# Moving two of the first loads of a four-layer attention kernel from SyncE's queue to ScalarE's

## The chip, the cores and the metric

The kernel runs on one core of one Trainium2 chip. The metric is the time of one execution on the device in microseconds (us); less is better. A core has five engines that work side by side and wait for each other through semaphores: TensorE (PE, matrix products; its weight loads are listed as PEld), VectorE (DVE), ScalarE (ACT), GpSimd (POOL) and SyncE (SP). Each takes its instructions in program order. In this kernel SP only issues DMA transfers. A transfer that an engine issues goes into that engine's queue (q1 for SP and q10 for ScalarE in the profile) and is carried out by the core's 16 DMA engines.

## The reference

The input x has 2048 rows of 512 numbers in bfloat16. Four layers follow one another, A, B, A, B, each as x = x + layer(layernorm(x)):

```python
def _A_ref(x, wqkv, w_phi, wo):            # 32 heads of 16
    q, k, v = split(x @ wqkv)
    pq, pk = q @ w_phi, k @ w_phi          # per head
    phi_q = concat(softmax(pq), softmax(-pq))
    phi_k = concat(softmax(pk), softmax(-pk))
    kv, z = phi_k^T v, sum(phi_k)
    return (phi_q kv / (phi_q z + 1e-6)) @ wo
...
def _B_ref(x, wqkv, wo):                   # window of 8 keys, every second one
    ...
    return (softmax(q kg / 4) vg) @ wo
```

Only the first 20 us or so matter for the change: layer norm of the first rows, and the preparation of layer A's weights.

## The kernel before, in words

The 2048 rows are cut into four blocks of 512 (`self.x[0]` to `self.x[3]`), and a block into four tiles of 128 rows. Every piece of work is a small function, put into a list with a stage and an engine by `step`. `run` then calls these functions in an order written out by hand: each word of the text `_ORDER` is a number, in base 36, of one list (the lists are numbered as they are first named), and stands for the next function of that list. So a word's place in `_ORDER` fixes where its instructions stand in their engine's queue. Places of two engines relative to each other in the text mean nothing, except that the tile buffers are handed out in this order, from the text `_SLOTS`.

What happens at the start, with the lines of the profile:

- **Loads** (`s_loads`). SP issues, one after the other: the first half of the key weights (`lraw(1, 0)`, L349, 256 KB, into the tile `wraw`), tiles 0 and 1 of x's first block (`lx0`, L337, 128 KB each), the second half of the key weights (`lraw(1, 1)`), the first half of the query weights (`lraw(0, 0)`), x's second block (`lx(1)`, L340, 512 KB), the second half of the query weights (`lraw(0, 1)`), tile 2 of x's first block, the value weights (`lv`, L343, 512 KB), tile 3, and later the rest. ScalarE issues one load in `setup`, behind its table load: the small tensor w_phi (L325, `phis`, 16 KB in runs of 32 bytes).
- **Products of zeros** (`warm`, L309). PE multiplies the zeroed tile `kvT` by itself 14 times: 11 times before its first real work, and three times between the first groups of real work. Nothing reads the result.
- **Folding w_phi into the weights** (`s_fold`). q @ w_phi is x @ (wq w_phi). So PE transposes the raw weights (`tr(pr)`, L386, eight transposes of 128x128 for each half), an engine copies the result to the tile `wT` (`ev`, L202 on DVE, L204 on ACT), PE multiplies it by the block-diagonal `PHI` (`mm(m)`, L396, four products for each m), and an engine copies that to `WA` (`ev2`, L202 or L204). Stage `fold1` does the key weights, `fold0` the query weights. `PHI` is made from `phis` on DVE (L274).
- **Layer norm** of the first block (`s_ln_first`, `s_norm`): DVE takes the statistics of a tile (`stat`, L515 and L516), ACT makes the reciprocal standard deviation (L450, L453), DVE or ACT applies it (L466, L468), PE transposes the tile (`pt`, L482), an engine copies the transposed tile out (L202 or L204).
- **Keys** (`s_a1`, `mk(t)`, L632): for each tile four products with the four 128-row pieces `WA[:, k]` of the folded key weights, so the fourth product of the first tile needs the last of the four copies by `ev2`. ACT takes the exponentials (L638).

PE's order there is: products 1 to 11, `fold1` transposes of the first half, products 12 and 13, `fold1` transposes of the second half, transposes of tile 0, product 14, `fold0` transposes of the first half, the 16 products by `PHI` of `fold1` with the transposes of tile 1 among them, `fold0` transposes of the second half, then `mk(0)` and `mk(1)`.

Of the kernel before, what the change touches and what calls it, by code (L numbers as in the profile page):

```python
# [60 lines left out]
8 2 i 2e 2p 23 i a i i 9 i i i i i i i 4e 1m i 0 0 f i e c j b 2 k 3 4 j o 1m l 3 m p 1n 0 i 1 n 1t o 1o q 1m 1p
r 0 1m 1u s 1m z z z 5 1m 1r 7 6 z 20 20 7 1q 1s 1t 21 21 t 20 20 1v 22 10 z 22 1t 7 1t 20 1w 22 t 11 24 24 13 u
12 16 12 1t t 15 1t v 12 12 22 x 18 14 1x d w w 1y 2c y 18 18 26 18 2d 1f 2d 2c 1z 2d 24 2d 27 17 19 18 1a 1b 21
1c 1d 22 21 22 39 1e 20 20 22 39 25 2c 3b 3a 3a 1f 3a 2d 3a 2f 2c 1f 1f 39 22 2f 2d 2g 1g 29 1f 2d 1j 2f 2d 7 1h
29 1i 1k 3a 29 2n 29 2i 2n 3c 2o 2o 2o 2k 2o 2k 2q 1l 2h 2n 2a 2k 2f 2n 2k 3a 2o 2j 24 2q 2r 2q 2o 2o 2o 29 2y
28 2y 2y 3c 2l 2z 2v 2z 2s 2z 2z 2k 2y 2z 39 36 31 2z 36 2z 3a 3b 36 36 2v 31 2v 37 2v 31 2t 36 2z 36 2b 2b 2b
2b 2m 2m 36 36 2m 3a 2w 2m 2v 33 34 32 31 3c 35 2q 3c 36 3b 2x g 2x 2u 2x 30 37 2x 36 38 38 38 38 3i 3c 3h 3c 39
3b 3a 3j 3k 3k 3k 3c 3d 3c 3e 3l 3b 3m 3d 3e 5h 3n 3m 3c 3e 3e 3l 5i 3o 3m 3q 3p 3m 3m 4f 3r 3m 3d 3l 5j 3e 3e
3s 3m 5i 3t 3m 3u 3m 3v 3d 3e 3e bd 5h 5m 5n 5k 5i 5l 5i 5i 3m 3d 3e 7c 5h 7d 5p 5i 5o 5i 5i 5r 3f 3g 3g 5q 5i
3f 3g 5i 3w 3f 3z 3x 3f 3g 5s 3y 7e 40 41 3g 7d 5u 5v 7f 5t 3g 41 42 41 41 44 3g 43 3g 43 5w 5x 5x 7f 45 46 43  # L70
43 47 43 7f 5y 3f 90 47 48 49 3g 4c 91 5x 41 4b 41 41 41 4a 92 5x 4d 60 91 4l 5z 61 5z 93 5z 4q 62 5z 4g 7d 4g
4g 4m 4q 63 5z 7d 4r 93 4i 4l 63 66 64 67 7g 4s 7j 65 7h 7i 4h 4j 7k bo 4n 4q 4q 4u 4w 91 7l 4t 7l 7l 7m 7l 7o
68 7n 7n 4l 7p 3h 7n 7q 4w 93 4v 7n 4v 91 4f 6a 7r 4o 6b 7n 6k 6f 69 4g 4k 4l 7r 6l 7s h 4w 6g 6k 6m 4p 6a 6c 6p
7t 7u 6a 6k 6f 6n 7v 4w 6k 6h 94 6r 6d 4x 4x b2 6r 4x 97 6o 98 4x 95 6f 69 7x 96 99 99 9a 4y 6i 99 7w 9b 6q 9c
6q 9d 9b 9b 99 9e 9b 6r 6a 6e 6f 6j 83 84 d4 6q 7y 9f 7y 9b 6r 6s 6s 6s 6s 9f 9h 9i 4y 9g 4w 8d 80 9j 7z 6t 6t
88 6s 83 89 6t 88 88 88 8a 8b 8f 8c 7y 6r 7x 4x 9l 6u 9k 6u 4y 6u 4w 6q 6u 83 85 83 86 87 81 9r 9w 7y 9w 9s 9x
4v 82 4v 9w 6v 9y 9z 4z a1 6v 4z 6v 6w 4z 8e 6v 4z 6y 9m 6x 6z 70 9n 70 70 71 72 73 70 9m 74 72 72 8e 9m 50 50
50 75 50 9o 72 51 9r 52 76 53 8f 54 55 72 9p 9w 76 8f 79 55 77 7a 9r 9t 55 58 78 7b 9u 55 9r 56 9m 8f 59 8g 57
5a 57 8e 8g a3 8g 8g 57 bz b0 8e 9q 57 9v a0 5b 57 8h a3 5b bz 8h a3 8g 5d c0 5e 5c 5f c0 c0 b0 c0 bz 8h b1 5g
b3 b1 8f b0 b1 b3 a2 b1 a4 c0 b1 a4 b1 a3 a4 a2 a4 b4 b5 a5 bz a5 8i 8i c0 8i a2 b3 a4 a2 c0 bx b6 c0 b3 a5 by  # L80
bx by by b0 b7 bx by by by a3 8i bx 8j 8j b1 8j 8l a6 8k 8j 8m b1 8n ap by aq aq ap a6 aq aq 8o 8o 8p by 8r 8o
8o 8q 8s 8q as 8t 8q as ap 8q au as ap a6 8u 8q a7 aq at 8u 8w aq bz a7 8v a7 aq aq 8x 8y 8z bx a9 a6 a7 a8 b8
aa as ax b8 ab ac ac c0 aw by ad ac ac b8 ax b8 ae be af av ah bb bb bb b9 ag ae bb b8 bf ae ae c1 ai bc bc ae
bc ar be ax bc bc bc bc bc ax ay ai aj ac ak am ac an ac al ac be bm ao bn bm bj bn bm bn bp ax bn bu bu bu c2
bu bj bj bn bg c2 c1 bm bn be az az bv bn az az ba bj ba ba bn bu bk bu ba bj bu bu c1 c2 c2 c2 c1 bp c2 bl bl
bh bl bu bq bp bp br bi bv bl bw bw bs bu iw bt bw bw c2 c7 c8 ix c9 c2 c9 c1 c2 c9 ca c3 cb iw cc cb fp c4 ca
fq c3 cd cb c4 ca cf ce cb cb cg cb c4 fr c4 ch cb cj e0 fq c3 fs fs ci cb cb c3 fs c5 c4 c4 c4 ck cb c4 cl e1
e2 cm c3 e1 e0 cp cn co e3 e1 e6 e4 e1 cq e5 e0 c4 e1 e1 c5 cq e8 e7 e1 e1 e9 ea cq e1 cr e1 eb cu h9 ee ct ec
ef fq cq fq ed eg cs cs cv cs cs ha eh eg ft hb fu fv eg ha hc hc fw hc eg fx fy fy cw el fy ei cs cw cy cx cq
cq d0 ej ek cq d1 cq ei fy d2 fz cz ei ei g3 df df em g1 df g0 ei em eo dh c6 da ep d3 en eq dg g2 di df dj g0  # L90
d5 ha d5 g0 d4 d6 da g0 g4 er dk d5 dk ha db g0 dc g4 es g6 hd d8 hh he da i7 dk d5 hf hg hi dl g5 g7 d7 d9 i7
g8 hi hj dd hi hl hk hk hm hi hn hk hk ho hk ho hp et hr f3 eu et da ey dl ev ey ey hs de hq dl f4 f1 et dl ez
ey ht ew f2 f0 f3 f5 f3 dm g9 f8 dm dm f6 dm dn dk i1 dn fa i1 fa i2 i3 dl i6 i6 gq f3 f7 f9 es i6 i9 et i6 i9
i6 i6 f9 dm hu ex fa ga i9 ia dn id i6 hv i1 fb fb fa fb fb fc i4 i1 i5 i6 dl c6 i6 do fc i9 ie ib i6 do hw hx
do fb gg i6 f9 fc gl i6 i6 i6 gm i6 ic hu i8 dp i6 ic dp dr dp dq gh ds ic hw f9 gg gg ic gi hy ic ic gl ic gl
ic fa gn gb ic ic do fd fd c5 ic go ic ic hw hw ic hz gb fd ic dp gc fe i0 gj gs fe gd fe if dt ff if if fh ig
gb if ig gg ig gl gs ge gs fg ig gk gb gp gt gr gr gr gt ga gf ih ih if ig if ig du gr if if gs ih du ig dv gt
ii gt dw fd ig ij ij ii ik gu gu ij du gt du ij dy ik ih gu fe gs dz il gv fi gv ii ij ij im ik il fj fk fj dx
in fl iq fj ir fj dx fo iq fm is ii gw gw ij gv il ij gx ik gw il io gv gv fn fm iy gz iq ip iq iu it gy iv it
h2 gw h0 gw h2 iz h3 h4 h5 h3 h1 h2 h6 h3 h2 h3 h5 h7 h5 h8 iy h5 j0  # L100
"""


# [33 lines left out]
class _Fast:  # L137
# [177 lines left out]
    def setup(self):  # L315
        nc, const = self.nc, self.const
        nc.scalar.preload_act_table_set("natural_log_exp_and_others")
# [4 lines left out]
        self.phis = const.tile([P, NB, DH], BF16, name="phis")
        self.x = [const.tile([P, 4, D], BF16, name="x%d" % b) for b in range(4)]
        with nc.allow_non_contiguous_dma(reason="tiny w_phi load"):
            nc.scalar.dma_start(out=self.phis[:], in_=self.A_w_phi.rearrange("(hb hl) d f -> (hl d) hb f", hb=NB))  # L325
# [4 lines left out]

    def s_loads(self):
        nc, add = self.nc, self.step
        wav = self.A_wqkv.rearrange("(m p) c -> p m c", p=P)
        xv = self.A_x.rearrange("b (j p) d -> p (b j) d", p=P)

        def lx0(t):
            nc.sync.dma_start(out=self.x[0][:, t, :], in_=xv[:, t, :])  # L337

        def lx(b):
            nc.sync.dma_start(out=self.x[b][:], in_=xv[:, 4 * b:4 * b + 4, :])  # L340
# [4 lines left out]
        def lraw(qk, h):
            if qk not in self.wraw:
                self.wraw[qk] = self.med([NB, D], "wraw")
            c = qk * D + h * 256
            nc.sync.dma_start(out=self.wraw[qk][:, :, h * 256:(h + 1) * 256], in_=wav[:, :, c:c + 256])  # L349
# [1776 lines left out]
```

## Time and profile before

| | |
|---|---|
| three runs | 319.18, 319.34, 319.43 us, median 319.34 us |
| the profiled execution | 319.68 us, its span (first to last instruction) 317.9 us |
| PE busy | 307.5 us (97%) |
| DVE busy | 295.1 us (93%) |
| ACT busy | 275.2 us (87%) |
| POOL busy | 47.1 us (15%) |
| DMA | 36.37 MB, mean 114 GB/s |

The profile is one execution. A line of its time line gives start and length in us, the engine, the line of the program, the operation, the tile written and the tiles read, the count, and in brackets how long the engine had been idle before it and what ended the wait. `SPq` and `ACTq` are the issues of transfers by SyncE and ScalarE; the transfer itself lands later. Lengths of matrix products are modelled and overlap: 11 products of 0.63 us stand in 4.88 us.

### The profile page before, as it was taken

Reading aid. Unit: us, or ns where it says so; the run is one execution under the profiler, and the core shown is the slowest. Engines: PE = TensorE matmul, PEld = TensorE weight load, DVE = VectorE, ACT = ScalarE, POOL = GpSimd, SP = SyncE. Lnnn points to the kernel's source line nnn. Section 1 sums busy time; section 2 is a strip of 40 time slices with the busy share of each in tenths; the row PEclk is TensorE's granted clock in tenths of the full one; section 3 lists DMA queues with packets and bytes.
Section 4 is the critical chain, followed back from the end, with each engine's and each line's share of the span. In section 5 each row is a group of like instructions: output and inputs, shape, how many; then the busy total and the mean of one; then the engine's idle time right before and its main releaser. Section 6 shows DMA issues by size and latency. Waiting matters only on the chain.

```text
span 317.9 us, 8896 instructions
## 1 busy us (share of the span) xinstructions
PE 307.5 (97%) x3578; PEld 153.0 (48%) x3578; DVE 295.1 (93%) x459; ACT 275.2 (87%) x639; POOL 47.1 (15%) x60
## 2 busy tenths in 40 slices
PE   8999999899999999999999999988999999999994
PEld 4654456445454444444444455544454544444552
DVE  6999996898999999999999999699998999999994
ACT  3999999999888778999999999899999867788761
POOL 6000000000003212000000000027011644045000
PEclk9999999999999999999999999999999999999999
DMA  6986200005694989569895500005189885565954
GB/s 199 345 203 143 41 2 4 2 19 142 150 191 96 157 141 139 99 106 151 140 131 71 69 0 2 4 19 134 49 195 137 134 157 119 103 181 122 163 148 170
DMA packets 45789, 36.37 MB, mean 114 GB/s; under 512 B 30832, under 2 KB 41136, under 8 KB 45744
## 3 DMA queue, kind: packets, MB, share of 16 engines
q1 hardware_dynamic: 45216, 35.75, 56.5%
q8 instruction: 29, 0.48, 0.7%
q14 instruction: 16, 0.13, 0.2%
q10 hardware_dynamic: 528, 0.02, 0.1%
HBM read 11.13 MB, written 3.25 MB: 45 GB/s over the span
## 4 chain that ended last, share of the span: by engine, by line
PE 88%; ACT 5%; DVE 2%; DMA 2%; SPq 1%; issue 1%; DVEq 0%; ACTq 0%
PE PS L967 23%; PE PS L553 18%; PE PS L632 9%; PE PS L644 9%; PE PS L737 6%; PE PS L1128 4%; PE PS L1066 4%; PE PS L1185 2%; DMA wraw<-in_A_wqkv_dram 2%; PE PS L707 2%; ACT Eq L745 2%; PE PS L482 1%; PE PS L940 1%; PE PS L556 1%; PE PS L1200 1%; PE PS L1082 1%
## 5 line engine op out<-in xcount | busy, mean ns | idle before, releaser
L967 PE MATMUL PS<-xnT,WB 128*128 128x512 bf16 x336 | 76.6, 380 | 0.0
L1059 DVE TENSOR_TENSOR prod<-QT,K 128x4096 bf16<-128x4096 bf16 x28 | 63.3, 2285 | 0.5 <-POOL K L993 0.5
L1121 DVE TENSOR_TENSOR pav<-PT,Vg 128x4096 bf16<-128x4096 bf16 (+1 forms) x29 | 62.9, 2213 | 0.2
L967 PEld LDWEIGHTS <-WB 128*128 128x128 bf16 x336 | 37.3, 114 | 36.3 <-issue 3.1
L745 ACT ACTIVATE Eq<-PS 128x512 bf16<-128x512 f32 x64 | 36.3, 619 | 0.0
L638 ACT ACTIVATE Ek<-PS 128x512 bf16<-128x512 f32 x64 | 35.1, 623 | 0.2 <-PE PS L632 0.2
L553 PEld LDWEIGHTS <-oT 128*128 128x128 bf16 x236 | 21.9, 98 | 26.6 <-issue 1.3
L737 PE MATMUL PS<-xnT,WA 128*128 128x512 bf16 x128 | 32.0, 380 | 0.5 <-DVE s L829 0.3
L578 ACT ACTIVATE sqd<-x 128x512 bf16<-128x512 bf16 x48 | 30.0, 635 | 2.1 <-DVE x L571 2.0
L644 PE MATMUL PS<-WA,xnT 128*128 128x512 bf16 x128 | 31.6, 379 | 0.0
L571 DVE SCALAR_TENSOR_TENSOR x<-PS,x 128x512 bf16<-128x512 f32 x46 | 30.1, 683 | 0.7 <-PE PS L553 0.7
L632 PE MATMUL PS<-WA,xnT 128*128 128x512 bf16 x128 | 30.7, 379 | 0.0
L204 ACT CAST oT<-PS 128x512 bf16<-128x512 f32 (+1 forms) x50 | 26.8, 600 | 3.6 <-PE PS L1128 2.1
L553 PE MATMUL PS<-WoA,oT 128*128 128x512 bf16 x128 | 29.8, 380 | 0.0
L553 PE MATMUL PS<-WoB,oT 128*128 128x512 bf16 x108 | 26.5, 379 | 0.0
L204 ACT CAST K<-PS 128x512 bf16<-128x512 f32 x30 | 17.3, 594 | 3.0 <-PE PS L967 1.9
L632 PEld LDWEIGHTS <-xnT 128*128 128x128 bf16 x128 | 12.4, 98 | 14.8 <-issue 0.4
L644 PEld LDWEIGHTS <-xnT 128*128 128x128 bf16 x128 | 12.3, 98 | 14.4 <-issue 0.4
L690 DVE TENSOR_TENSOR Ek<-Ek,rk 128x4096 bf16<-128x4096 bf16 (+1 forms) x10 | 18.6, 1859 | 0.4 <-ACT rk L685 0.4
L737 PEld LDWEIGHTS <-WA 128*128 128x128 bf16 x128 | 11.7, 98 | 14.6 <-issue 1.7
L466 DVE TENSOR_SCALAR xn<-x,rstd,nmr 128x512 bf16<-128x512 bf16 x48 | 17.5, 412 | 0.5
L204 ACT CAST V<-PS 128x512 bf16<-128x512 f32 x26 | 15.2, 596 | 2.9 <-PE PS L967 2.9
(175 smaller groups left out, 506.4 us busy)
## 6 DMA issues: line engine op xcount, KB each, us to landing
Vg<-V SPq DMA_DIRECT2D x112, 131.5 KB, 4.7
Prho<-rd SPq DMA_DIRECT2D x8, 512.0 KB, 5.3
x<-in_A_x_dram SPq DMA_DIRECT2D x3, 512.0 KB, 6.8
WB<-in_B_wqkv_dram SPq DMA_DIRECT2D x3, 512.0 KB, 9.6
out_dram<-x SPq DMA_DIRECT2D x6, 256.0 KB, 2.3
wraw<-in_A_wqkv_dram SPq DMA_DIRECT2D x4, 256.0 KB, 4.2
vd<-Vs SPq DMA_DIRECT2D x2, 272.0 KB, 3.0
x<-in_A_x_dram SPq DMA_DIRECT2D x4, 128.0 KB, 3.6
```

The source lines that it names most:

```text
L204: self.nc.scalar.copy(out=out, in_=in_)
L553: nc.tensor.matmul(y[:], lhsT=lh(t, c), rhs=Wo()[:, c, :], start=(c == 0), stop=(c == NB - 1 and not onpe))
L571: nc.vector.scalar_tensor_tensor(out=xb[:, t, :], in0=T[t][:], scalar=1.0, in1=xb[:, t, :], op0=ALU.mult, op1=ALU.add, **kw)
L578: nc.scalar.activation(out=sqd[:], in_=xb[:, t, :], func=ACT.Square, accum_out=T["ss"][:, t:t + 1])
L632: nc.tensor.matmul(pk[:], lhsT=xnT[:, t, k, :], rhs=self.WA[:, k, D:2 * D], start=(k == 0), stop=(k == NB - 1))
L638: nc.scalar.activation(out=T["E"][:, t, s, :], in_=T["k", t][:], func=ACT.Exp, scale=1.0 - 2.0 * s)
L644: nc.tensor.matmul(pv[:], lhsT=xnT[:, t, k, :], rhs=self.WA[:, k, 2 * D:3 * D], start=(k == 0), stop=(k == NB - 1))
L737: nc.tensor.matmul(pq[:], lhsT=self.WA[:, k, hb * P:(hb + 1) * P], rhs=xnT[:, :, k, :], start=(k == 0), stop=(k == NB - 1))
L745: nc.scalar.activation(out=self.Eq[L, b][s][:, :, hb, :], in_=T[hb][:].rearrange("p (t i) -> p t i", t=4), func=ACT.Exp, scale=1.0 - 2.0 * s)
L967: nc.tensor.matmul(pp[:], lhsT=self.WB[:, k, i * D + c:(i + 1) * D:NB], rhs=xnT[:, :, k, :], start=(k == 0), stop=(k == NB - 1))
L1059: nc.vector.tensor_tensor(out=pr[:], in0=QT[:, c:c + 1, :].to_broadcast([P, NW, TB]), in1=win, op=ALU.mult)
L1121: nc.vector.tensor_tensor(out=pv, in0=PT[:, :, lo:lo + n].unsqueeze(1).to_broadcast([P, NB, 2, n]), in1=vw, op=ALU.mult)
```

## The change

Two loads are issued by ScalarE, behind the load of w_phi, and no longer by SP: tile 0 of x's first block, and the second half of the key weights. The load of w_phi itself moves from `setup` to a step of its own, and is still ScalarE's first transfer. SP's other loads stay in their order and close up.

```diff
+    "raw_act": ((1, 1),),
...
-        with nc.allow_non_contiguous_dma(reason="tiny w_phi load"):
-            nc.scalar.dma_start(out=self.phis[:], in_=self.A_w_phi.rearrange("(hb hl) d f -> (hl d) hb f", hb=NB))
...
+        def lphi():
+            with nc.allow_non_contiguous_dma(reason="tiny w_phi load"):
+                nc.scalar.dma_start(out=self.phis[:], in_=self.A_w_phi.rearrange("(hb hl) d f -> (hl d) hb f", hb=NB))
+
         def lx0(t):
-            nc.sync.dma_start(out=self.x[0][:, t, :], in_=xv[:, t, :])
+            q = nc.scalar if t == 0 else nc.sync
+            q.dma_start(out=self.x[0][:, t, :], in_=xv[:, t, :])
...
-            nc.sync.dma_start(out=self.wraw[qk][:, :, h * 256:(h + 1) * 256], in_=wav[:, :, c:c + 256])
+            q = nc.scalar if (qk, h) in _OPT["raw_act"] else nc.sync
+            q.dma_start(out=self.wraw[qk][:, :, h * 256:(h + 1) * 256], in_=wav[:, :, c:c + 256])
...
         for t in range(4):
-            add("ld_x0", "SP", lx0, t)
+            add("ld_x0", "SP" if t else "ACT", lx0, t)
+        add("ld_phi", "ACT", lphi)
...
-                    add("ld_raw%d" % qk, "SP", lraw, qk, h)
+                    add("ld_raw%d" % qk, "ACT" if (qk, h) in _OPT["raw_act"] else "SP", lraw, qk, h)
```

The whole text `_ORDER` changes, since three lists are new and every number behind them grows. Read back into steps, what differs is this:

- The first loads stand at the head of the text. ScalarE: w_phi, tile 0, second half of the key weights. SP: first half of the key weights, tile 1, first half of the query weights, x's second block, second half of the query weights, tile 2, value weights, tile 3, and on as before.
- PE: ten products of zeros (not eleven) stand before the `fold1` transposes of the first half, one (not two) between these and the transposes of the second half, and two behind them, before the transposes of tile 0. All 14 are still there.
- The order of every other step on its engine is as before. The text `_SLOTS` has one letter at another place, so that the second `wraw` tile, which is now named earlier, gets the buffer that it had.

More of the change, by code (lines that the diff above doesn't have):

```diff
@@ L60 @@
 _ORDER = """
[L61 to L100, printed above, removed]
+2 4 0 1 5 6 7 6 1 3 b l 2h 2s 26 l d l l c l l l l l l 4h 1p l i h f m e n m r 1p l l o p s 1q l q 1w r 1r t 1p
@@ new lines @@
+1s u 1 1p 1x v 1p 12 12 12 8 1p 1u a 9 12 23 23 a 1t 1v 1w 24 24 w 23 23 1y 25 13 12 25 1w a 1w 23 1z 25 w 14 27
+27 16 x 15 19 15 1w w 18 1w y 15 15 25 10 1b 17 20 g z z 21 2f 11 1b 1b 29 1b 2g 1i 2g 2f 22 2g 27 2g 2a 1a 1c
+1b 1d 1e 24 1f 1g 25 24 25 3c 1h 23 23 25 3c 28 2f 3e 3d 3d 1i 3d 2g 3d 2i 2f 1i 1i 3c 25 2i 2g 2j 1j 2c 1i 2g
+1m 2i 2g a 1k 2c 1l 1n 3d 2c 2q 2c 2l 2q 3f 2r 2r 2r 2n 2r 2n 2t 1o 2k 2q 2d 2n 2i 2q 2n 3d 2r 2m 27 2t 2u 2t 2r
+2r 2r 2c 31 2b 31 31 3f 2o 32 2y 32 2v 32 32 2n 31 32 3c 39 34 32 39 32 3d 3e 39 39 2y 34 2y 3a 2y 34 2w 39 32
@@ new lines @@
+39 2e 2e 2e 2e 2p 2p 39 39 2p 3d 2z 2p 2y 36 37 35 34 3f 38 2t 3f 39 3e 30 j 30 2x 30 33 3a 30 39 3b 3b 3b 3b 3l
+3f 3k 3f 3c 3e 3d 3m 3n 3n 3n 3f 3g 3f 3h 3o 3e 3p 3g 3h 5k 3q 3p 3f 3h 3h 3o 5l 3r 3p 3t 3s 3p 3p 4i 3u 3p 3g
+3o 5m 3h 3h 3v 3p 5l 3w 3p 3x 3p 3y 3g 3h 3h bg 5k 5p 5q 5n 5l 5o 5l 5l 3p 3g 3h 7f 5k 7g 5s 5l 5r 5l 5l 5u 3i
+3j 3j 5t 5l 3i 3j 5l 3z 3i 42 40 3i 3j 5v 41 7h 43 44 3j 7g 5x 5y 7i 5w 3j 44 45 44 44 47 3j 46 3j 46 5z 60 60
+7i 48 49 46 46 4a 46 7i 61 3i 93 4a 4b 4c 3j 4f 94 60 44 4e 44 44 44 4d 95 60 4g 63 94 4o 62 64 62 96 62 4t 65
@@ new lines @@
+62 4j 7g 4j 4j 4p 4t 66 62 7g 4u 96 4l 4o 66 69 67 6a 7j 4v 7m 68 7k 7l 4k 4m 7n br 4q 4t 4t 4x 4z 94 7o 4w 7o
+7o 7p 7o 7r 6b 7q 7q 4o 7s 3k 7q 7t 4z 96 4y 7q 4y 94 4i 6d 7u 4r 6e 7q 6n 6i 6c 4j 4n 4o 7u 6o 7v k 4z 6j 6n 6p
+4s 6d 6f 6s 7w 7x 6d 6n 6i 6q 7y 4z 6n 6k 97 6u 6g 50 50 b5 6u 50 9a 6r 9b 50 98 6i 6c 80 99 9c 9c 9d 51 6l 9c
+7z 9e 6t 9f 6t 9g 9e 9e 9c 9h 9e 6u 6d 6h 6i 6m 86 87 d7 6t 81 9i 81 9e 6u 6v 6v 6v 6v 9i 9k 9l 51 9j 4z 8g 83
+9m 82 6w 6w 8b 6v 86 8c 6w 8b 8b 8b 8d 8e 8i 8f 81 6u 80 50 9o 6x 9n 6x 51 6x 4z 6t 6x 86 88 86 89 8a 84 9u 9z
@@ new lines @@
+81 9z 9v a0 4y 85 4y 9z 6y a1 a2 52 a4 6y 52 6y 6z 52 8h 6y 52 71 9p 70 72 73 9q 73 73 74 75 76 73 9p 77 75 75
+8h 9p 53 53 53 78 53 9r 75 54 9u 55 79 56 8i 57 58 75 9s 9z 79 8i 7c 58 7a 7d 9u 9w 58 5b 7b 7e 9x 58 9u 59 9p
+8i 5c 8j 5a 5d 5a 8h 8j a6 8j 8j 5a c2 b3 8h 9t 5a 9y a3 5e 5a 8k a6 5e c2 8k a6 8j 5g c3 5h 5f 5i c3 c3 b3 c3
+c2 8k b4 5j b6 b4 8i b3 b4 b6 a5 b4 a7 c3 b4 a7 b4 a6 a7 a5 a7 b7 b8 a8 c2 a8 8l 8l c3 8l a5 b6 a7 a5 c3 c0 b9
+c3 b6 a8 c1 c0 c1 c1 b3 ba c0 c1 c1 c1 a6 8l c0 8m 8m b4 8m 8o a9 8n 8m 8p b4 8q as c1 at at as a9 at at 8r 8r
@@ new lines @@
+8s c1 8u 8r 8r 8t 8v 8t av 8w 8t av as 8t ax av as a9 8x 8t aa at aw 8x 8z at c2 aa 8y aa at at 90 91 92 c0 ac
+a9 aa ab bb ad av b0 bb ae af af c3 az c1 ag af af bb b0 bb ah bh ai ay ak be be be bc aj ah be bb bi ah ah c4
+al bf bf ah bf au bh b0 bf bf bf bf bf b0 b1 al am af an ap af aq af ao af bh bp ar bq bp bm bq bp bq bs b0 bq
+bx bx bx c5 bx bm bm bq bj c5 c4 bp bq bh b2 b2 by bq b2 b2 bd bm bd bd bq bx bn bx bd bm bx bx c4 c5 c5 c5 c4
+bs c5 bo bo bk bo bx bt bs bs bu bl by bo bz bz bv bx iz bw bz bz c5 ca cb j0 cc c5 cc c4 c5 cc cd c6 ce iz cf
@@ new lines @@
+ce fs c7 cd ft c6 cg ce c7 cd ci ch ce ce cj ce c7 fu c7 ck ce cm e3 ft c6 fv fv cl ce ce c6 fv c8 c7 c7 c7 cn
+ce c7 co e4 e5 cp c6 e4 e3 cs cq cr e6 e4 e9 e7 e4 ct e8 e3 c7 e4 e4 c8 ct eb ea e4 e4 ec ed ct e4 cu e4 ee cx
+hc eh cw ef ei ft ct ft eg ej cv cv cy cv cv hd ek ej fw he fx fy ej hd hf hf fz hf ej g0 g1 g1 cz eo g1 el cv
+cz d1 d0 ct ct d3 em en ct d4 ct el g1 d5 g2 d2 el el g6 di di ep g4 di g3 el ep er dk c9 dd es d6 eq et dj g5
+dl di dm g3 d8 hd d8 g3 d7 d9 dd g3 g7 eu dn d8 dn hd de g3 df g7 ev g9 hg db hk hh dd ia dn d8 hi hj hl do g8
@@ new lines @@
+ga da dc ia gb hl hm dg hl ho hn hn hp hl hq hn hn hr hn hr hs ew hu f6 ex ew dd f1 do ey f1 f1 hv dh ht do f7
+f4 ew do f2 f1 hw ez f5 f3 f6 f8 f6 dp gc fb dp dp f9 dp dq dn i4 dq fd i4 fd i5 i6 do i9 i9 gt f6 fa fc ev i9
+ic ew i9 ic i9 i9 fc dp hx f0 fd gd ic id dq ig i9 hy i4 fe fe fd fe fe ff i7 i4 i8 i9 do c9 i9 dr ff ic ih ie
+i9 dr hz i0 dr fe gj i9 fc ff go i9 i9 i9 gp i9 if hx ib ds i9 if ds du ds dt gk dv if hz fc gj gj if gl i1 if
+if go if go if fd gq ge if if dr fg fg c8 if gr if if hz hz if i2 ge fg if ds gf fh i3 gm gv fh gg fh ii dw fi
@@ L101 @@
+ii ii fk ij ge ii ij gj ij go gv gh gv fj ij gn ge gs gw gu gu gu gw gd gi ik ik ii ij ii ij dx gu ii ii gv ik
+dx ij dy gw il gw dz fg ij im im il in gx gx im dx gw dx im e1 in ik gx fh gv e2 io gy fl gy il im im ip in io
+fm fn fm e0 iq fo it fm iu fm e0 fr it fp iv il gz gz im gy io im h0 in gz io ir gy gy fq fp j1 h2 it is it ix
+iw h1 iy iw h5 gz h3 gz h5 j2 h6 h7 h8 h6 h4 h5 h9 h6 h5 h6 h8 ha h8 hb j1 h8 j3
 """
@@ L113 @@
     "med": (
-        "b79ca642352f85de6b0464b12833892cb7516e70efd8561f1706ed4a53bc7430e3f9eba731d9c0411a4091d20483b8ae4cf4"
+        "b679ca42352f85de6b0464b12833892cb7516e70efd8561f1706ed4a53bc7430e3f9eba731d9c0411a4091d20483b8ae4cf4"
         "b71d6236f9ec40bfd6ea7830c4"
```

## Prediction

> **What bounds the kernel now.** First the chain of waits of the whole span, then the same chain in order of time for the first 40 us.
>
> ```profile
> PE 88%; ACT 5%; DVE 2%; DMA 2%; SPq 1%; issue 1%; DVEq 0%; ACTq 0%
> ```
>
> ```profile
> 0.92 0.46 SPq L349
> ...
> 4.01 6.41 DMA wraw<-in_A_wqkv_dram
> 10.43 0.05 issue
> 10.47 0.62 PE PS L386 x8
> ```
>
> Past 10.47 us the chain is nearly all PE. Before it stand SP's issues one behind the other and then one transfer, the second half of the query weights, issued at 4.01 and landed at 10.43. So whatever moves this start should move the end by as much: nothing later in the chain hangs on an outside clock. Next, the time line of each engine.
>
> ```profile
> 0.92 0.46 SPq L349 DMA_DIRECT2D wraw<-in_A_wqkv_dram  x1
> 1.42 0.97 SPq L337 DMA_DIRECT2D x<-in_A_x_dram  x2
> 2.44 0.98 SPq L349 DMA_DIRECT2D wraw<-in_A_wqkv_dram  x2
> 3.46 0.51 SPq L340 DMA_DIRECT2D x<-in_A_x_dram  x1
> 4.01 0.51 SPq L349 DMA_DIRECT2D wraw<-in_A_wqkv_dram  x1
> ```
>
> ```profile
> 0.88 1.28 ACT L317 ACT_TABLE_LOAD   x1 [0.88 <-PEq L2110]
> 0.91 0.48 ACTq L325 DMA_DIRECT2D phis<-in_A_w_phi_dram  x1
> 5.50 0.29 ACT L450 ACTIVATE lnv<-mv,eps_t 128x1 f32<-128x1 f32 x1 [3.35 <-DVE mv L516]
> ...
> 8.82 0.59 ACT L204 CAST WA<-PS 128x512 bf16<-128x512 f32 x1 [0.30 <-PE PS L396]
> ...
> 9.78 1.58 ACT L204 CAST WA<-PS 128x512 bf16<-128x512 f32 x3
> 11.21 1.07 ACT L204 COPY wT<-PS 128x1024 bf16<-128x1024 bf16 x1
> ```
>
> ```profile
> 4.56 0.69 DVE L515 BATCH_NORM_STATS2 stat<-x 128x6 f32<-128x512 bf16 x1 [1.75 <-DMA x<-in_A_x_dram]
> ...
> 6.96 0.66 DVE L202 COPY wT<-PS 128x1024 bf16<-128x1024 bf16 x1
> ...
> 7.72 0.69 DVE L202 COPY wT<-PS 128x1024 bf16<-128x1024 bf16 x1
> ```
>
> ```profile
> 1.34 4.88 PE L309 MATMUL PS<-kvT 128*128 128x512 bf16 x11 [1.34 <-DVE kvT L264]
> 6.01 0.78 PE L386 MATMUL PS<-ident,wraw 128*128 128x128 bf16 x8
> 6.63 0.59 PE L309 MATMUL PS<-kvT 128*128 128x512 bf16 x2
> 7.06 0.61 PE L386 MATMUL PS<-ident,wraw 128*128 128x128 bf16 x8
> 7.73 0.38 PE L309 MATMUL PS<-kvT 128*128 128x512 bf16 x1
> ...
> 9.01 0.83 PE L396 MATMUL PS<-PHI,wT 128*128 128x128 bf16 x12
> 10.47 0.62 PE L386 MATMUL PS<-ident,wraw 128*128 128x128 bf16 x8 [0.63 <-DMA wraw<-in_A_wqkv_dram]
> 10.93 1.89 PE L632 MATMUL PS<-WA,xnT 128*128 128x512 bf16 x8
> ```
>
> Two separate chains meet at PE near 10.5 us. One is the transfer above: PE was through at 9.84 (9.01 + 0.83) and idled 0.63 us for it. The other starts when **tile 0 of x lands**: DVE, idle for 1.75 us, begins at 4.56 and is then busy nearly throughout (5.08 of the 5.50 us from 4.90 on, in the table below), and its copies of `wT` (to 8.41) let PE make the folded weights, which ACT copies out from 8.82 until 11.36 (9.78 + 1.58) without a pause. The second chain is nearly as late as the first. A key product is one seventh of 1.89 - 0.38 us, 0.216 us, behind the one before, so the fourth, the first that needs ACT's last copy, starts at 10.93 + 3 x 0.216 = 11.58. ACT was done at 11.36: 0.22 us of slack, 0.18 if 0.04 us are left for the signal (10.43 to 10.47 above).
>
> **The change part by part.** *SP's issues close up.* SP's issues stand 0.5 us apart (0.92, 1.42, then two from 2.44). Two of those ahead of 4.01 go to ScalarE, so the second half of the query weights is issued about 1.0 us earlier, at 3.0. Does it land 1.0 earlier? The DMA engines in stretches:
>
> ```profile
> core 0: us, PE busy (x) PEld busy (x) DVE busy (x) ACT busy (x) POOL busy (x), PEclk, DMA share, GB/s
> 2.60:3.20 0.60, 0.60 (x3) 0.30 (x2) 0.20 (x3) 0.00 (x0) 0.45 (x3) 1.00 1.12 284
> 3.20:3.80 0.60, 0.60 (x3) 0.15 (x1) 0.00 (x0) 0.00 (x0) 0.48 (x3) 1.00 1.18 311
> 3.80:4.90 1.10, 1.10 (x4) 0.46 (x3) 0.34 (x1) 0.00 (x0) 0.87 (x5) 1.00 0.68 194
> 4.90:10.40 5.50, 4.95 (x55) 3.44 (x52) 5.08 (x13) 3.98 (x10) 1.77 (x10) 1.00 1.03 323
> ```
>
> They are full except from 3.80 to 4.90, where they move 194 GB/s instead of 311 and are 0.68 busy. The bytes ahead of this transfer are the same after the change, so what can be won is that hollow: 1.1 x (1 - 194/311) = 0.41 us. Bounds: nothing, if the hollow stays; 1.0, if the issue alone decided. I take 0.40, the row with the rates being the nearest: landing at 10.03, transposes from 10.07.
>
> A rule speaks against even this. The Trainium skill, "DMA: Bandwidth & Descriptors", section "Issuing engines are not separate DMA queues", says that transfers issued by several engines run on the same 16 DMA engines and interleave, and that only the issuing time is saved. By it the gain lies in the hollow and nowhere else. The trace agrees where the share is 1.03; it shows no run with two busy queues.
>
> *Tile 0 of x on ScalarE's queue.* ScalarE issues w_phi at 0.91 while its table load runs, so at 0.5 us a piece tile 0 goes out at 1.4, when SP issued it before, and the second key half at 1.95 instead of 2.44. ScalarE has nothing else until 5.50 (idle 3.35 us), so the two issues themselves cost nothing. What changes is what stands ahead of the tile: no longer 256 KB of key weights, but w_phi's 528 small packets.
>
> ```profile
> q10 hardware_dynamic: 528, 0.02, 24.7%
> ```
>
> This is ScalarE's queue from 2.6 to 3.8 us (packets, MB, share of 16 engines): w_phi's whole transfer lies there, starting 1.7 us after its issue. Call d the shift of the tile's landing. Before, its bytes were the last 128 KB of about 384 KB and done near 3.7 (the 284 and 311 GB/s rows), 0.86 us before DVE started. If it may now follow w_phi's first packets, 1.4 + 1.7 = 3.1 and 128 KB at 311 GB/s (0.42 us) give 3.5: d = -0.2. If it starts when w_phi is half through, near 3.3, and shares the engines with tile 1 from SP, it needs twice 0.42 us: 4.1, d = +0.4. If it waits for w_phi's last packet at 3.8 and shares, 4.64: d = +0.9. I take +0.1, midway between the first two; the third needs the worst on every DMA engine.
>
> *What PE makes of both.* The transposes start at the later of 10.07 and PE's being free, 9.84 + d, so 0.40 us earlier. The fourth key product needs ACT's last copy, 11.36 + d, plus 0.04; it stood at 11.58. So PE's shift is the larger of -0.40 and d - 0.18, which for d = +0.1 is -0.08 us. ACT's copy of `wT` at 11.21 shifts by d as well and ends at 12.28 + d, before PE needs it at 12.66 (10.93 + 8 x 0.216). If this cover of 0.38 us were used up, d would be paid in full from there on.
>
> *The product of zeros.* The first transposes start one product earlier, at 5.6 (4.88 us for 11, 0.43 us each). The `wT` copy that waits for them stands at 6.96 behind DVE's own work, and the transposes are over at 6.79 already: worth nothing. The other transposes end at 7.67, the copy stands at 7.72: that cover is thin, and coming earlier only helps if d is negative. They may start near 6.7 if their half has landed:
>
> ```profile
> DMA to landing us min/median/max: 3.2/4.2/6.4
> ```
>
> By the median of the four weight halves it lands at 1.95 + 4.2 = 6.15, by the longest at 8.4, which would cost 0.7 us through that copy; the longest belongs to the half issued last, into the fullest queue, so I take the median and no cost. Tile 0's transposes get two products ahead of them in place of two plus the eight transposes: nothing.
>
> *Sum.* 319.68 for the profiled execution, less 0.08: 319.60. That execution lies 0.34 above the median of 319.34, so the forecast for the median is 319.26, told as 319.3. A quarter of a per mille is far inside 0.2% (0.64 us), which is about what a measurement of this kernel can tell from no change.
>
> **The rivals.** *Faster, tile 0 lands early.* If ScalarE's queue is served beside SP's from the first packet at 2.6, the tile's bytes are there by about 3.05, and d is -0.65. Then PE's shift is bounded by its own chain and the landing: with the landing moved by the whole 1.0 to 9.4, PE free at 9.2, the larger of -1.03 and -0.83: 318.5. For it: DVE's 1.75 us of idle time. Against it: w_phi's packets lie ahead in the same queue, and the DMA engines are full from 2.6 on. Both gains must be near their ends together; below d = -0.46 it would pass 0.64.
>
> *Slower, tile 0 behind w_phi.* This is the third case above: d = +0.9, all of DVE's and ACT's chain late by that, PE late by 0.72, and 320.1. It decides from d = +0.82. For it: the last of w_phi's packets run until 3.8, and tile 1 and two weight halves compete from both queues. Against it: w_phi takes 24.7% of the engines in that stretch, 0.3 us of each if it runs alone.
>
> *Slower, TensorE's clock.* Eleven products ran 0.43 us apart, the two at 6.63 only 0.21 (0.59 - 0.38). So PE doubles its pace near 6.4 us, while the first transposes run. After the change those stand half a microsecond further ahead. If this put the doubling off, PE would have four products and 40 transposes or small products left at half pace; 4 x 0.21 plus 40 x 0.056 (0.61 - 0.22 over seven steps) is 3.1 us at full pace, so up to 3.1 more, and nothing if the doubling came at once. I take the middle less the 0.4 of waiting for the weights, about 1.2: 320.6. The granted clock stands at 1.00 in every row and doesn't show this step. The rule of the Trainium skill, "TensorE: Matmul & The Clock Gate", Part 4, that a transpose doesn't count as busy time as a product does, is what would bring it about; the doubling in this trace came during transposes, but behind five microseconds of products.
>
> **How the numbers follow.** Forecast, no change: 0.62. Tile 0 early: 0.20. Tile 0 behind w_phi: 0.10. Clock: 0.08. So faster 0.20, same 0.62, slower 0.18. Within the forecast d from -0.3 to +0.5 gives 318.9 to 319.7. The range goes on to the fast rival at 318.5, with half of that case above it, and just below the slow one, 320.0; about one case in ten is left out at each side.
>
> **What would show it.** SP's issue of the second query half near 3.0, and its transposes at 10.0 to 10.1. DVE's first statistics near 4.7, and ACT's last copy of the folded key weights near 11.5, with the fourth key product waiting for it. The first transposes at 5.6, still followed by products 0.21 us apart. The hollow between 3.8 and 4.9 filled. I am wrong if DVE starts before 4.1 or after 5.3, if products after the first transposes are still 0.43 apart, or if the shift at 12 us is not found again at the end.

## The result, and the profile after

| | before | after |
|---|---|---|
| median (range), six runs each on the same chip | 319.39 us (319.18 to 319.60) | 322.48 us (321.64 to 323.46) |
| ratio, 95% interval | | 1.0096 [1.0079, 1.0113] |
| the profiled execution, its span | 319.68 us, 317.9 us | 323.04 us, 321.3 us |

The changed kernel is slower by 3.1 us. The forecast of 319.3 us is wrong, and so is the range, which ended at 320.0.

Its chain of waits by engine, and then the same chain in order of time:

```profile
PE 77%; DVE 9%; ACT 8%; DMA 2%; issue 2%; ACTq 0%; DVEq 0%
```

```profile
1.42 0.60 ACTq L341
...
2.05 6.81 DMA wraw<-in_A_wqkv_dram
8.86 0.05 issue
8.91 0.68 PE PS L392 x8
9.59 0.85 PE PS L310 x2
```

The transfer in the chain is no longer the second half of the query weights (landed at 10.43 us before) but the second half of the key weights. ScalarE issued it at 2.05 us and it landed 6.8 us later, at 8.86; on SP's queue it had been issued at 2.44 and had landed 4.1 us later, and its transposes had started at 7.06 without a wait. The time line, with the edited lines a few numbers further down than before:

```profile
0.91 0.48 ACTq L337 DMA_DIRECT2D phis<-in_A_w_phi_dram  x1
1.42 0.60 ACTq L341 DMA_DIRECT2D x<-in_A_x_dram  x1
2.05 0.46 ACTq L354 DMA_DIRECT2D wraw<-in_A_wqkv_dram  x1
...
2.99 0.51 SPq L354 DMA_DIRECT2D wraw<-in_A_wqkv_dram  x1
...
5.23 0.69 DVE L521 BATCH_NORM_STATS2 stat<-x 128x6 f32<-128x512 bf16 x1 [2.42 <-DMA x<-in_A_x_dram]
...
5.58 0.78 PE L392 MATMUL PS<-ident,wraw 128*128 128x128 bf16 x8
6.19 0.38 PE L310 MATMUL PS<-kvT 128*128 128x512 bf16 x1
...
8.91 0.68 PE L392 MATMUL PS<-ident,wraw 128*128 128x128 bf16 x8 [2.34 <-DMA wraw<-in_A_wqkv_dram]
9.38 1.06 PE L310 MATMUL PS<-kvT 128*128 128x512 bf16 x2
...
10.24 0.63 PE L488 MATMUL PS<-ident,xn 128*128 128x128 bf16 x4
...
13.74 0.61 PE L392 MATMUL PS<-ident,wraw 128*128 128x128 bf16 x8
...
14.72 1.73 PE L638 MATMUL PS<-WA,xnT 128*128 128x512 bf16 x7 [0.37 <-ACT WA L205]
```

PE idles 2.34 us for the second half of the key weights. Behind it the two products of zeros start 0.43 us apart (1.06 less the 0.63 of a single one), where the two at 6.63 us before stood 0.21 apart: PE works at half pace. The key products start at 14.72, 3.8 us later than the 10.93 of before. The stretches of the changed kernel show the clock and the DMA engines:

```profile
core 0: us, PE busy (x) PEld busy (x) DVE busy (x) ACT busy (x) POOL busy (x), PEclk, DMA share, GB/s
3.80:4.90 1.10, 1.10 (x4) 0.45 (x3) 0.00 (x0) 0.00 (x0) 0.87 (x5) 1.00 1.08 319
...
9.00:9.50 0.50, 0.50 (x9) 0.50 (x9) 0.00 (x0) 0.00 (x0) 0.00 (x0) 0.83 1.09 383
9.50:12.50 3.00, 3.00 (x22) 2.18 (x21) 1.32 (x3) 0.59 (x1) 0.00 (x0) 0.50 1.06 330
12.50:13.00 0.50, 0.50 (x9) 0.50 (x8) 0.50 (x2) 0.38 (x1) 0.00 (x0) 0.76 1.01 338
13.00:13.50 0.50, 0.50 (x11) 0.49 (x9) 0.48 (x1) 0.50 (x2) 0.00 (x0) 1.00 1.00 264
```

First row: the hollow of the DMA engines is filled as forecast, 319 GB/s instead of 194. The others: the granted clock is 0.50 from 9.33 (0.83 in a half microsecond is a third of it at 0.50) to 12.74, which is 3.4 us. In the profile of before, the rows of the same stretch show 1.00.

Why did the half take so long on a shorter queue? The packets of the two queues in two stretches, 4.25 to 6.00 us and then 6.00 to 8.75 us, and last those of ScalarE's queue alone from 7.65 to 8.50 us (packets, MB, share of 16 engines):

```profile
q1 hardware_dynamic: 525, 0.30, 58.0%
q10 hardware_dynamic: 476, 0.24, 49.0%
...
q1 hardware_dynamic: 1185, 0.92, 100.9%
q10 hardware_dynamic: 74, 0.04, 4.3%
...
q10 hardware_dynamic: 13, 0.01, 2.4%
```

Until 6.0 us the two queues share the engines nearly by halves, and all of the half's 0.26 MB is there but the last 74 packets with 0.04 MB. Those are spread over most of the next 2.75 us, while SP's queue fills the engines. The last 13 start about 0.065 us apart and take about 0.025 us each (2.4% of 16 engines over 0.85 us, divided by 13): that fits a single engine that serves a packet of SP's queue between two of them, though the trace doesn't name the engines. The half landed only behind the last of these, so it waited for a thin tail.

### The profile page after: what moved, and what is told of

The parts are those of the page before. It is cut to its first block, busy times and chain, and to the rows that moved or that the text cites. A ratio compares the mean times of both kernels' runs of the same rounds, so it can differ in the third digit from the quotient of the medians.

```text
span 321.3 us, 8868 instructions
## 1 busy us (share of the span) xinstructions
PE 306.8 (95%) x3549; PEld 154.3 (48%) x3578; DVE 295.4 (92%) x459; ACT 275.2 (86%) x639; POOL 47.0 (15%) x60
## 4 chain that ended last, share of the span: by engine, by line
PE 77%; DVE 9%; ACT 8%; DMA 2%; issue 2%; ACTq 0%; DVEq 0%
PE PS L973 17%; PE PS L559 15%; PE PS L638 9%; PE PS L650 8%; PE PS L743 6%; PE PS L1134 4%; PE PS L1072 3%; DVE prod L1065 3%; PE PS L1191 2%; DMA wraw<-in_A_wqkv_dram 2%; ACT Eq L751 2%; PE PS L713 2%; PE PS L488 1%; DVE Eq L881 1%; PE PS L562 1%
## 5 line engine op out<-in xcount | busy, mean ns | idle before, releaser
L650 PE MATMUL PS<-WA,xnT 128*128 128x512 bf16 x121 | 30.7, 379 | 0.5 <-issue 0.2
L638 PE MATMUL PS<-WA,xnT 128*128 128x512 bf16 x123 | 30.0, 379 | 0.6 <-ACT WA L205 0.4
L559 PE MATMUL PS<-WoA,oT 128*128 128x512 bf16 x120 | 29.1, 380 | 0.4
```

The source lines that it names most:

```text
L559: nc.tensor.matmul(y[:], lhsT=lh(t, c), rhs=Wo()[:, c, :], start=(c == 0), stop=(c == NB - 1 and not onpe))
L638: nc.tensor.matmul(pk[:], lhsT=xnT[:, t, k, :], rhs=self.WA[:, k, D:2 * D], start=(k == 0), stop=(k == NB - 1))
L650: nc.tensor.matmul(pv[:], lhsT=xnT[:, t, k, :], rhs=self.WA[:, k, 2 * D:3 * D], start=(k == 0), stop=(k == NB - 1))
```

## The experiments

Loads are named in the order of their queue: K1, K2 and Q1, Q2 are the halves of the key and query weights, t0, t1, t2 the tiles of x's first block, x1 its second block, v the value weights, phi is w_phi. Theory A is that the half of the key weights lands late because ScalarE's queue issues it; A2 is the form that A took after the first runs: the last of ScalarE's two big loads is late, whichever it is, because SP's closed-up loads compete with it. The main rival was the clock: fewer products ahead of the first transposes hold the pace down. Ratios are to the kernel before on the same chip, with 95% intervals.

**Tile 0 alone on ScalarE's queue** (K2 back on SP).

```diff
-    "raw_act": ((1, 1),),
+    "raw_act": (),
...
-SP: K1 t1 Q1 x1 Q2 t2 v     ScalarE: phi t0 K2
+SP: K1 t1 K2 Q1 x1 Q2 t2 v  ScalarE: phi t0
```

> Only tile 0 of x is issued by ScalarE; the second half of the key weights goes back to SP, third in line behind the first half and tile 1. Products of zeros as in the changed kernel. Theory A (the loss comes from the second key half: on ScalarE's queue it landed 6.8 us after its issue, PE waited 2.3 us for it, and worked at half pace for some microseconds after that wait): the wait is gone, products after the first transposes stay 0.21 us apart, time 319.4 to 320.0, the remainder being tile 0, which DVE got 0.67 us later (5.23 against 4.56). Theory B (the late tile 0 behind w_phi is what costs): most of the 3.1 us stays, 321.5 or more.

319.89 us, ratio 1.0001 [0.9988, 1.0015]. DVE starts at 4.97 us, the second key transposes at 6.05. By itself, tile 0's move costs nothing that these runs can tell.

**The key half alone on ScalarE's queue** (t0 back on SP).

```diff
-SP: K1 t1 Q1 x1 Q2 t2 v     ScalarE: phi t0 K2
+SP: K1 t0 t1 Q1 x1 Q2 t2 v  ScalarE: phi K2
```

> Only the second half of the key weights is issued by ScalarE (second there, behind w_phi); tile 0 of x stays with SP. Products of zeros as in the changed kernel. Theory A: PE waits for this half as in the changed kernel, 1.5 us or more, and the time is 321.0 to 323. Theory B: DVE starts near 4.6 again and the time is back to 319.3 to 319.8.

319.65 us, ratio 1.0003 [0.9994, 1.0013]: theory A as it stood fails. Time line, and the queues from 3.50 to 5.25 us and from 5.25 to 8.75 us:

```profile
1.41 0.61 ACTq L357 DMA_DIRECT2D wraw<-in_A_wqkv_dram  x1
...
5.70 0.61 PE L395 MATMUL PS<-ident,wraw 128*128 128x128 bf16 x8
```

```profile
q10 hardware_dynamic: 692, 0.27, 57.6%
q1 hardware_dynamic: 394, 0.31, 57.3%
...
q1 hardware_dynamic: 1733, 1.23, 111.4%
```

The half lands 4.2 us after its issue, as the forecast had it, and ScalarE's queue has no packet left after 5.25: no tail. So the loss needs both loads on ScalarE's queue.

**Only the product of zeros moved**, with the loads of before.

```diff
-SP: K1 t1 Q1 x1 Q2 t2 v        ScalarE: phi t0 K2
+SP: K1 t0 t1 K2 Q1 x1 Q2 t2 v  ScalarE: phi
```

> All loads of x and of the raw weights by SP as before the change; only the place of the products of zeros is that of the changed kernel. Theory A: no wait, 319.2 to 319.6. Theory C (the transposes that stand one product earlier put off the doubling of PE's pace): products behind the first transposes 0.43 us apart, 320.3 to 321.

319.66 us, ratio 0.9997 [0.9987, 1.0006], just above the range expected and no slower than before; products behind the second transposes 0.21 us apart. The place of the products costs nothing, and the clock rival of the prediction is out.

**Only the loads moved**, with PE's order of before.

```diff
-PE: 10 products, K1 transposes, 1 product, K2 transposes, 2 products
+PE: 11 products, K1 transposes, 2 products, K2 transposes
```

> The loads of the changed kernel with the products of zeros in the old order: eleven ahead of the first transposes, two between these and the next. Theory A: the wait is for the same transfer, so 320 to 323 with the scatter of the changed kernel; PE's idle time is 0.2 us shorter by the one product more. Rival: the place of the products is what brings the loss, 319.3 to 319.9.

320.46 us, ratio 1.0026 [1.0014, 1.0039]. The half landed 6.2 us after its issue and PE waited 0.87 us:

```profile
8.25 0.62 PE L395 MATMUL PS<-ident,wraw 128*128 128x128 bf16 x8 [0.87 <-DMA wraw<-in_A_wqkv_dram]
```

The loads alone bring a loss. It is smaller than in the first six runs of the changed kernel, which is what the next run is about.

**The changed kernel again.**

> The changed kernel itself, on the same chip as the three others of this set. It should take 321.6 to 323.5 again, with PE waiting near 2 us for the second key half. What it settles besides: whether its runs with a granted clock of 1.00 lie about 1 us below those with 0.993, as the first six did (321.64 and 321.66 against 322.46 to 323.46).

320.81 us (319.77 to 322.85), ratio 1.0045 [1.0020, 1.0070], so below the range expected. Its profiled execution:

```profile
8.26 0.62 PE L392 MATMUL PS<-ident,wraw 128*128 128x128 bf16 x8 [1.24 <-DMA wraw<-in_A_wqkv_dram]
8.72 0.59 PE L310 MATMUL PS<-kvT 128*128 128x512 bf16 x2
```

The half landed 6.2 us after its issue instead of 6.8, PE waited 1.24 us, and no half pace followed. So the same program lands its half at different times. Of the 15 runs of the changed kernel so far, the nine with a mean clock of 0.997 or more lie at 319.77 to 321.87 us (median 320.81), the six at 0.993 to 0.995 at 322.46 to 323.46 (median 322.78). Four of these six are among the first six runs, two among the nine of this set.

**The key half ahead of tile 0 on ScalarE's queue.**

```diff
-SP: K1 t1 Q1 x1 Q2 t2 v  ScalarE: phi t0 K2
+SP: K1 t1 Q1 x1 Q2 t2 v  ScalarE: phi K2 t0
```

> ScalarE issues w_phi, then the second key half, then tile 0: the same two loads as in the changed kernel, swapped. The kernel with the key half alone on ScalarE took 319.65 and had no wait, the one with tile 0 alone 319.89. Theory A2 (the key half is late in the changed kernel because its packets, issued third at 2.05, meet SP's query half and x's second block on the same engines and alternate with them): issued at 1.42 it lands before these start, PE doesn't wait, and only tile 0 is later: 319.6 to 320.6. Theory D (two big loads in ScalarE's queue are too many, in whatever order): PE still waits over 1 us, 321 or more.

322.19 us, ratio 1.0073 [1.0048, 1.0098]: the expectation is right on the half and missed the time, since the tile's price was mis-sized.

```profile
6.83 0.69 DVE L524 BATCH_NORM_STATS2 stat<-x 128x6 f32<-128x512 bf16 x1 [4.02 <-DMA x<-in_A_x_dram]
...
6.86 0.68 PE L395 MATMUL PS<-ident,wraw 128*128 128x128 bf16 x8
7.38 0.59 PE L313 MATMUL PS<-kvT 128*128 128x512 bf16 x2
```

Now the transposes don't wait for data, and tile 0 starts DVE 2.27 us later than the 4.56 of before. The late one is the last on ScalarE's queue.

**x's second block issued later on SP's queue.**

```diff
-SP: K1 t1 Q1 x1 Q2 t2 v  ScalarE: phi t0 K2
+SP: K1 t1 Q1 Q2 t2 x1 v  ScalarE: phi t0 K2
```

> The changed kernel, but SP issues x's second block (512 KB in packets of 1 KB) behind the second half of the query weights (packets of 512 bytes) and tile 2. In the changed kernel the key half's last packets went out two per 0.1 us between x's, until 8.5 us. Theory A2: with shorter packets between them, or with none of x's yet, they are out 0.5 to 1 us sooner, PE's wait shrinks from 2.3 to 1.3 to 1.9 us, time 321 to 322; if the packets of SP's queue don't matter, the wait stays at 2.3 and the time at 322 to 323.

320.19 us, ratio 1.0017 [1.0007, 1.0026]. The half takes 5.5 us to land, the last packets on ScalarE's queue are over by 7.0, and PE waits 1.94 us (the first transposes had started early, at 4.83):

```profile
7.58 0.62 PE L395 MATMUL PS<-ident,wraw 128*128 128x128 bf16 x8 [1.94 <-DMA wraw<-in_A_wqkv_dram]
```

That fits A2, with a time below the range expected, but it isn't proof: it is one profile against 6.2 to 6.8 us in four profiles with the changed kernel's loads, and the interval of the ratio overlaps with that of the changed kernel run beside it.

**The key half late on SP's own queue**, nothing but phi on ScalarE's.

```diff
-SP: K1 t1 Q1 x1 Q2 t2 v        ScalarE: phi t0 K2
+SP: K1 t0 t1 Q1 x1 K2 Q2 t2 v  ScalarE: phi
```

> No load by ScalarE but w_phi: SP issues all, with the second key half behind x's second block (it is then issued near 3.5 instead of 2.4 and has all of that block ahead of it), products of zeros as in the changed kernel. If the loss is only that the half lands late, whichever queue it is on, PE waits 2 us or more for it here too, the pace halves afterwards, and the time is 321.5 to 323.5. If ScalarE's queue itself is what costs (its issues, or two queues at once), 319.4 to 320.5.

323.36 us, ratio 1.0113 [1.0095, 1.0132]. A late landing by itself makes a loss of this size, without a big load on ScalarE's queue:

```profile
9.18 1.03 PE L395 MATMUL PS<-ident,wraw 128*128 128x128 bf16 x8 [2.95 <-DMA wraw<-in_A_wqkv_dram]
10.01 1.06 PE L313 MATMUL PS<-kvT 128*128 128x512 bf16 x2
```

**What does the half pace cost?** Products of zeros in PE's wait keep PE busy: 11 in the changed kernel, and 11, 8 and 5 in the kernel just above.

```diff
-    "warm": 14,
+    "warm": 25,
...
-PE: 10 products, K1 transposes, 1 product, K2 transposes, 2 products
+PE: 10 products, K1 transposes, 12 products, K2 transposes, 2 products
```

(22 and 19, with 9 and 6 products there, in the other two.) First the changed kernel with 11:

> The changed kernel with eleven more products of zeros behind the first transposes, 11 x 0.216 = 2.4 us at full pace, so that PE has work while it waits for the second key half. The wait itself can't get shorter. Theory A in two parts: the half-landing wait costs about 1.9 us (those transposes began at 8.91 and not at 7.06), and the rest, about 1.2 us, is PE's lower pace after standing idle; so this kernel keeps its products 0.21 us apart, the mean granted clock at 1.00, and takes 321.0 to 321.7, with less scatter than the 321.64 to 323.46 of the changed kernel. If the idle time has nothing to do with the pace: 322 to 323.5, products after the wait still 0.43 us apart.

322.54 us, ratio 1.0084 [1.0056, 1.0112], clock 1.00, and not the 321 expected. Here the 12 products themselves held PE for some 0.6 us. The half landed 6.5 us after its issue at 2.05, near 8.6, and the transposes started behind the products, at 9.18, without a wait:

```profile
6.43 2.91 PE L313 MATMUL PS<-kvT 128*128 128x512 bf16 x12
...
9.18 0.61 PE L395 MATMUL PS<-ident,wraw 128*128 128x128 bf16 x8
```

Then the other kernel with 11:

> The kernel with the second key half issued late by SP (323.36 us, all four runs with a granted clock of 0.992 to 0.995, PE's wait 2.95 us), with eleven more products of zeros, 2.4 us, put into that wait. They end before the half lands, so the wait for the data stays as it is, and only PE's idle time goes. Theory A (half a microsecond of idle time is harmless, near three are answered with half pace for 3.4 us): clock 0.997 or more, products behind the wait 0.21 us apart, 322.2 to 322.7, about 0.8 below. If the pace isn't tied to the idle time: 323.2 to 323.5 again.

323.15 us, ratio 1.0099 [1.0075, 1.0122]. The pace is kept, DVE's statistics of the next block start 1.0 us ahead, and the end is no earlier: missed. PE's time line:

```profile
9.53 0.62 PE L395 MATMUL PS<-ident,wraw 128*128 128x128 bf16 x8 [1.49 <-DMA wraw<-in_A_wqkv_dram]
9.99 0.59 PE L313 MATMUL PS<-kvT 128*128 128x512 bf16 x2
...
299.28 1.02 PE L562 MATMUL PS<-WoB,oT 128*128 128x512 bf16 x4 [0.95 <-issue]
```

The lead over the kernel without the products is still 0.93 us at 291 us and is lost behind it; the last row has a wait of 0.95 us that ends on nothing the profile shows. The other two counts were to tell whether that is an accident:

> As late_sp (both of ScalarE's big loads back on SP, second key half behind x's second block) with 8 products of zeros in PE's wait instead of 11. Of the wait of 2.95 us some 1.2 us are left idle, so the pace stays at 0.21 us a product, and DVE's statistics of the second block's first tile start near 12.1 as with 11 products. With 11 the lead of 0.92 us over late_sp lasted until 297 us and was lost in one wait of PE of 0.95 us near 298 us that ends on nothing the profile shows. Theory H, the half pace costs about 0.9 us and that late wait is an accident of where the instructions lie: without it the end is 0.9 us before late_sp's 323.4, at 322.3 to 322.6, and no wait of that kind stands near 298 us. Theory N, the lead is always eaten near the end: 323.0 to 323.5, with PE waiting 0.6 to 1.0 us near 298 us again.

> The same with 5 products: some 1.9 us of the wait stay idle. By the earlier runs (idle 1.2 to 1.9 us, no half pace; 2.3 and 2.95, half pace) it lies at the edge: DVE's statistics of the second block's first tile start near 12.1 with full pace, near 13.1 with half pace. Theory H: 322.3 to 322.6 at full pace, 323.2 to 323.5 at half pace, unless the late wait is there. Theory N: 323.0 to 323.5 either way.

With 8 products 323.33 us, ratio 1.0103 [1.0088, 1.0119], with 5 products 321.98 us, ratio 1.0075 [1.0062, 1.0089]. The 5 first, then the 8:

```profile
10.10 0.62 PE L395 MATMUL PS<-ident,wraw 128*128 128x128 bf16 x8 [2.98 <-DMA wraw<-in_A_wqkv_dram]
10.55 0.59 PE L313 MATMUL PS<-kvT 128*128 128x512 bf16 x2
```

```profile
10.84 0.62 PE L395 MATMUL PS<-ident,wraw 128*128 128x128 bf16 x8 [3.22 <-DMA wraw<-in_A_wqkv_dram]
11.29 1.00 PE L313 MATMUL PS<-kvT 128*128 128x512 bf16 x2
```

Neither came out as expected, because the half landed later still in these executions, at 10.05 and 10.79 us, against 9.13 and 9.48 in the two kernels with the same loads. But they complete a table that answers the question. Shifts against the profiled execution of before: of the second key transposes (7.06 us), of a step of ScalarE at 20.91 us (L450, the second of its steps over four tiles at once), of its last `et` at 291.31 us (L1313), and of the whole time (319.68 us).

| kernel | pace after the wait | transposes | at 21 us | at 291 us | end |
|---|---|---|---|---|---|
| x's block later | full | +0.52 | +0.70 | +0.77 | +0.69 |
| changed, again | full | +1.20 | +1.36 | +1.42 | +1.26 |
| changed, 11 products | full | +2.12 | +2.27 | +2.26 | +2.68 |
| late on SP, 11 products | full | +2.47 | +2.64 | +2.78 | +3.68 |
| late on SP, 5 products | full | +3.04 | +3.21 | +3.33 | +3.63 |
| changed | half | +1.85 | +3.53 | +3.60 | +3.36 |
| late on SP | half | +2.12 | +3.66 | +3.71 | +3.45 |
| late on SP, 8 products | half | +3.78 | +5.36 | +5.46 | +5.96 |

From the transposes to 21 us the full pace adds 0.15 to 0.18 us, the half pace 1.54 to 1.68: it costs 1.4 to 1.5 us. From there to 291 us no shift changes by more than 0.15. In the last 25 us the four kernels of the table with 14 products win 0.1 to 0.3 us and the four with more lose 0.3 to 0.9. The added products alone don't explain that: the kernel with only the loads moved and the one with the key half ahead of tile 0 have 14 products too and lose 0.34 and 0.35 us there. Three of the four with more have a wait like the one at 299.28, of 0.95, 0.68 and 0.63 us; the one with 5 has none of that kind. What moves the last 25 us stays open.

**Tile 0 first on ScalarE's queue**, the version that the experiments point to: nothing big behind another load there, K2 ahead of x's block on SP.

```diff
-SP: K1 t1 Q1 x1 Q2 t2 v     ScalarE: phi t0 K2
+SP: K1 t1 K2 Q1 x1 Q2 t2 v  ScalarE: t0 phi
```

> ScalarE issues tile 0 of x first and w_phi second, nothing else; all other loads on SP in the old order. With w_phi ahead, the kernel with tile 0 alone on ScalarE gave DVE its start at 4.97 and took 319.89. Now the tile's packets lie ahead of w_phi's: DVE should start at 4.0 to 4.4, and if w_phi is there when DVE wants it, 0.9 us behind, the end moves 0.1 to 0.4 us ahead of the kernel before, 319.1 to 319.5, which five rounds may just tell. If the copies for the weights then wait for the second key half or PE's transposes, no change, 319.4 to 319.8.

319.15 us against 319.51 (21 runs of before), ratio 0.9986 [0.9974, 0.9997].

```profile
3.64 0.70 DVE L524 BATCH_NORM_STATS2 stat<-x 128x6 f32<-128x512 bf16 x1 [0.83 <-DMA x<-in_A_x_dram]
...
10.71 1.73 PE L641 MATMUL PS<-WA,xnT 128*128 128x512 bf16 x7 [0.37 <-ACT WA L208]
```

DVE starts 0.92 us earlier than before, ahead even of the 4.0 to 4.4 us expected, and the key products start 0.22 us earlier. It beats both kernels, the old one by hardly more than the measurement can tell.

## Why the prediction was wrong

**The step that failed** is the cost of the second key half, "By the median of the four weight halves it lands at 1.95 + 4.2 = 6.15", and "I take the median and no cost". It was issued at 2.05 and landed at 8.86. The reason given, that the longest time belongs "to the half issued last, into the fullest queue", took each queue by itself. The half was in the emptier queue, but the DMA engines served the other one beside it. Before, K2 stood ahead of Q1 and x1 on one queue, so their packets came behind its own; on two queues that order is gone. That both loads must be on ScalarE's queue and that the last of the two is the late one, the runs showed; that the tail shrinks when x1 goes later rests on one profile. That the tail is one engine or a few still taking turns with SP's packets is read from the spacing of the packets. No run tests it by itself, and why these engines lag behind the others stays open. The Trainium skill, "DMA: Bandwidth & Descriptors", section "Queues, rings and completion order", says that each engine takes its queues in turn, a packet at a time; the shares of 58.0% and 49.0% until 6.0 us agree.

**The price beside it failed too.** I let a landing at 8.4 cost "0.7 us through that copy". The transposes themselves come between, with 0.61 us, and PE stands still for the landing: 1.95 + 6.41 + 0.05 = 8.41, and less 7.06 that is 1.35. With the right price the longest landing would have made a rival of more than a microsecond.

**The half pace** was in the rivals, with the wrong trigger. It was not the place of the products (that kernel ran like before) but PE's idle time: 2.34 us in the changed kernel's profile, and 2.95 and 3.22 in two others, while 2.98 in a fourth brought none (the last section says what tells them apart). With the key half late on SP's queue, all four runs have a mean clock of 0.992 to 0.995; with 11 products in the wait, all eight runs of the two kernels have 0.997 or more. Its size, 1.4 to 1.5 us, is near the 1.2 that I took for that rival, but by luck: 1.2 came from the middle of a range from nothing to 3.1 (and on 319.34 it makes 320.5, not 320.6). So 3.53 us at 21 us is 1.85 of late landing, 0.17 that every kernel of the table with full pace shows as well, and some 1.5 of half pace. In the runs without it only the landing is paid. Together with the spread of the landing itself this fits the range from 319.77 to 323.46, of which two executions were profiled.

**Point by point.** SP's issue at 3.0: right (2.99). The hollow filled: right (319 GB/s), and useless, as what went first into it was not what PE needed next; the second query half's transposes moved from 10.47 to 13.74 and did not wait for it. Tile 0: d was 5.23 - 4.56 = +0.67, within its bounds and not the +0.1 taken; alone it cost nothing that shows (4.97 in that kernel). The forecast's rule for PE, d - 0.18, held where tile 0 was the late one: in the kernel with the key half first, d = 2.27 gives 2.09, and the shift at 21 us was 1.97. First transposes at 5.6: right (5.58), with no effect on the pace. ACT's last copy at 11.5: wrong, since all of it lay behind the key half. That a shift of the start is found again at the end: right, within 0.5 us from 21 us on for the kernels with 14 products. None of the three signs of being wrong watched the half that failed: DVE started before 5.3, the shift was there at the end, and products 0.43 us apart came only behind the second transposes.

## What to carry to other kernels

When loads move to a second queue, they no longer stand ahead of the loads left behind: draw up who shares the engines with the last load on the new queue, and take its longest landing, not the median, as the term of the sum. Here one small, urgent load at the head of the second queue won a little, and a big one behind it paid for the transfers that closed up. And a wait that opens on TensorE ahead of dense work has two prices, its length and the half pace that may follow.
